# Long convolution, gate and MLP on one core: ssm_k transposed as words of two time steps, small tables first, another order in each group, one DMA per output tile

## The chip, the core and the metric

The kernel runs on one core of a Trainium2 chip. A core has a matrix engine (TensorE, "PE" in the profile, with its weight loads listed as "PEld"), a vector engine (VectorE, "DVE"), a scalar engine (ScalarE, "ACT") and a general engine (GpSimd, "POOL"), each with an instruction stream of its own, and queues from which data transfers (DMA) are issued ("SPq", "ACTq"). They run beside each other and wait for each other by semaphores. TensorE takes its operands from the on-chip memory SBUF and writes to PSUM[...]; DVE or ACT then bring a result from PSUM to SBUF, which is called an eviction here.

The metric is the time of one execution on the device in microseconds (us), the median of several runs: 208.96 us before the change. The profile is of one execution, and its span of 207.0 us is a little shorter than the time of a run.

## What is computed

With S = 2048 time steps, D = 512 channels and a hidden width of 1376, all tensors in bf16:

```python
def _A_ref(q, k, v, shift_k, ssm_k, ssm_D):        # q is layernorm(x)
    k_shift = sum over t of k_pad[:, t:t + S, :] * shift_k[:, ks - 1 - t]   # four taps
    kv = k_shift * v
    y = causal convolution of kv with ssm_k along the 2048 steps, by FFT of length 2 * S
    y = y + kv * ssm_D
    return q * y

x = A_q
h = x + _A_ref(_layernorm(x), A_k, A_v, A_shift_k, A_ssm_k, A_ssm_D)
h2 = h + relu(_layernorm(h) @ B_w1) @ B_w2
```

The kernel does the long convolution as a two-stage transform: 2048 steps are split into 32 rows of 64, a first stage transforms along one index, a second along the other. ssm_k and kv each go through both, are multiplied, and go back. Before a first stage, the data, which lie with channels on the partitions, are transposed so that time lies there.

## The kernel before

The kernel is written with a manual schedule: each engine runs its instructions in the order of the program text. These are the parts that matter for the change. The line numbers in the profile are those of the whole kernel.

The tables of the second stage (`cs`, `cc`; `cn` is the negative of `cs`) are sines, made by DVE (turns, in integers) and ACT (the sine). They come ahead of the small tables of the first stage (`f1f`):

```python
    for a, t in cs:                                   # two pieces, of 22 and 10 of the 32 indices
        ks = slice(a, a + t.shape[1])
        nc.vector.tensor_tensor(out=tsn[:, ks, :], ..., op=ALU.add)
        wrap(tsn[:, ks, :], 8192)                     # bitwise and, on DVE
        for dp in range(2):
            table((a, t), tsn, dp)                    # Sin, on ACT
    ...                                               # turns t1, t3; f1f and dsc by _sin on ACT
    cc_turns(0)                                       # two DVE instructions each
    cc_turns(16)
    ...
    for rg in range(DC):                              # on GpSimd: tap weights as diagonal matrices
        nc.gpsimd.tensor_tensor(out=wdiag[:, rg, :, :], ...)
        if rg == 1: ...                               # f1hi, f1lo from f1f, on GpSimd
    ...                                               # f2hi, f2lo, then cn = -cs in four pieces, on GpSimd
```

ssm_k (`sk`) is transposed as single 16-bit values, eight 128 x 128 transposes to a PSUM tile, and each tile is evicted by DVE ("D") or ACT ("A") in turn:

```python
    def to_rows(src, q, fl, eng):
        shape = [P, 8, P]
        pst = tap_bank(q % 5 - 3, shape, BF16, "pst") if q % 5 > 2 else place(shape, BF16, "pst")
        for i in range(8):
            nc.tensor.transpose(out=pst[:, i, :], in_=src[:, :, :, 8 * q + i], identity=ident[:])   # L268
        copy(eng, fl[:, :, :, 8 * q:8 * q + 8], pst[:].rearrange("p i (d g) -> p g d i", d=2))

    for q in range(8):
        to_rows(skv, q, kfl, "DADADADA"[q])
```

Then eight groups follow. In each, the four taps of a part of k are summed on TensorE into two PSUM banks of their own and multiplied by v on DVE (the product kv is written into the memory of `sk`), and one eighth of the first stage of ssm_k is computed and evicted into `a1k`:

```python
    def taps(c, h):
        ...                                           # 2 x 4 matmuls of 512 columns, L332; 2 products on DVE, L335

    for gb in range(8):
        taps(gb // 2, gb % 2)
        stage1(kfl, a1k, gb, ("AA", "AD")[gb % 2], pairs=(gb == 2))   # matmuls L289; two evictions
        if gb in (0, 1, 3, 5):
            cc_part()                                 # one sine of table cc, on ACT
    pl.pop("psT")                                     # the two tap banks become a fourth place
    places.append(pl.push("psX", space=PSUM))
    ring[:] = [1, 3, 2, 0]                            # order in which the places are used next
```

kv is then transposed as 32-bit words, each two time steps, so with half as many transposes. This is the form that the change takes for ssm_k too:

```python
    for q in range(8):
        pst = place([P, 4, P], F32, "pst2")
        for i in range(4):
            nc.tensor.transpose(out=pst[:, i, :], in_=kv32[:, 4 * q + i, :], identity=ident32[:])     # L369
        if "DADDADAD"[q] == "D":
            nc.vector.tensor_single_scalar(out=xfl32[:, :, :, ms], in_=pst[:].bitcast(I32)..., scalar=0,
                                           op=ALU.bitwise_or)                                         # L372
        else:
            for d in range(2):
                nc.scalar.copy(out=xfl[:, :, d, 8 * q:8 * q + 8]..., in_=src[:, d])                   # L378
```

The second stage of ssm_k (`ps2k`, L307 and L309) comes next, then the first stage of kv, the products, the way back, the gate and the MLP. At the end each output tile of 128 rows is stored by four DMAs of 32 rows; the last tile is computed and stored in two halves of 256 columns, whose DMAs alternate between two queues:

```python
                nc.vector.scalar_tensor_tensor(out=o[:, 0:w], in0=ps2[:, 0:w], ...)                   # L725
                for a, dst in enumerate(_tokens(out_d, t, 1)):
                    if parts > 1:
                        dst = bass.AP(tensor=dst.tensor, offset=dst.offset + w * h, ap=[[64 * D, 32], [1, w]])
                    eng = nc.scalar if parts > 1 and a % 2 else nc.sync
                    eng.dma_start(out=dst, in_=o[32 * a:32 * a + 32, 0:w])                            # L731
```

Of the kernel before, what the change touches and what calls it, by code (L numbers as in the profile page):

```python
# [9 lines left out]
ALU = mybir.AluOpType  # L10
BF16 = mybir.dt.bfloat16
# [45 lines left out]
def kernel(  # L57
# [122 lines left out]
    def wrap(t, M):  # L180
        nc.vector.tensor_single_scalar(out=t, in_=t, scalar=M - 1, op=ALU.bitwise_and)

    def table(piece, turns, dp):
        a, t = piece
        nc.scalar.activation(out=t[:, :, 64 * dp:64 * dp + 64], in_=turns[:, a:a + t.shape[1], :], func=ACT.Sin,
                             scale=hsc[:, dp:dp + 1], bias=hbi[:, dp:dp + 1])

    for a, t in cs:
        ks = slice(a, a + t.shape[1])
        nc.vector.tensor_tensor(out=tsn[:, ks, :], in0=ta[:, ks].unsqueeze(2).to_broadcast([P, t.shape[1], 64]),  # L190
                                in1=ta[:, 32:96].unsqueeze(1).to_broadcast([P, t.shape[1], 64]), op=ALU.add)
        wrap(tsn[:, ks, :], 8192)
        for dp in range(2):
            table((a, t), tsn, dp)
# [12 lines left out]
    cc_parts = [(p, dp) for p in cc for dp in range(2)]  # L207

    def cc_turns(a):
        part = tcs[:, a:a + 16, :]  # L210
        nc.vector.tensor_single_scalar(out=part, in_=tsn[:, a:a + 16, :], scalar=2048.0, op=ALU.add)
        wrap(part, 8192)

    def cc_part():
        p, dp = cc_parts.pop(0)
        table(p, tcs, dp)
# [8 lines left out]
    for f in (f2hi, f2lo):  # L225
        nc.gpsimd.memset(f[:], 0.0)

    for rg in range(DC):
        nc.gpsimd.tensor_tensor(out=wdiag[:, rg, :, :], in0=ident[:].unsqueeze(1).to_broadcast([P, KS, P]),
                                in1=wsh[:, rg, :].unsqueeze(2).to_broadcast([P, KS, P]), op=ALU.mult)  # L230
        if rg == 1:
            nc.gpsimd.tensor_copy(out=f1hi[:, 0:64], in_=f1f[:])
            nc.gpsimd.tensor_tensor(out=f1f[:], in0=f1f[:], in1=f1hi[:, 0:64], op=ALU.subtract)
            nc.gpsimd.tensor_copy(out=f1lo[:, 0:64], in_=f1f[:])
# [4 lines left out]
    for a, b in ((0, 8), (8, 16), (16, 22), (22, 32)):  # L239
        (ao, to), (ai, ti) = [[p for p in tab if p[0] <= a][-1] for tab in (cn, cs)]  # L240
        nc.gpsimd.tensor_single_scalar(out=to[:, a - ao:b - ao, :], in_=ti[:, a - ai:b - ai, :].bitcast(F32), scalar=-1.0,
                                       op=ALU.mult)

    def copy(eng, o, i):
        if eng == "A":
            nc.scalar.copy(out=o, in_=i)  # L246
        else:
            nc.vector.tensor_copy(out=o, in_=i)  # L248
# [12 lines left out]
    def tap_bank(i, shape, dtype, name):  # L261
        return psum_t.tile(shape, dtype, tag=f"pk{i}", name=name)

    def to_rows(src, q, fl, eng):
        shape = [P, 8, P]
        pst = tap_bank(q % 5 - 3, shape, BF16, "pst") if q % 5 > 2 else place(shape, BF16, "pst")
        for i in range(8):
            nc.tensor.transpose(out=pst[:, i, :], in_=src[:, :, :, 8 * q + i], identity=ident[:])  # L268
        copy(eng, fl[:, :, :, 8 * q:8 * q + 8], pst[:].rearrange("p i (d g) -> p g d i", d=2))

    def stage1(fl, a_out, gb, engs, pairs=False):

# [38 lines left out]


    kfl = early.tile([P, 64, 2, 64], BF16, name="kfl")
    skv = sk[:].rearrange("p c (a b) -> p c a b", b=64)
# [7 lines left out]


    kvp2 = sk[:].rearrange("p c t -> p (c t)").rearrange("p (m c a e) -> p m c a e", m=32, c=DC, e=2)
    ident32 = early.tile([P, P], F32, name="ident32")
    nc.gpsimd.tensor_copy(out=ident32[:], in_=ident[:])
# [34 lines left out]
    pl.pop("kvp")  # L361
    xfp = pl.push("xfp", side="right")
    xfl = xfp.tile([P, 64, 2, 64], BF16, name="xfl")
    kv32 = sk[:].rearrange("p c t -> p (c t)").bitcast(F32).rearrange("p (m x) -> p m x", m=32)
    xfl32 = xfl[:].rearrange("p g d n -> p (g d n)").bitcast(I32).rearrange("p (g d m) -> p g d m", g=64, d=2)
    for q in range(8):
        pst = place([P, 4, P], F32, "pst2")
        for i in range(4):
            nc.tensor.transpose(out=pst[:, i, :], in_=kv32[:, 4 * q + i, :], identity=ident32[:])  # L369
        ms = slice(4 * q, 4 * q + 4)  # L370
        if "DADDADAD"[q] == "D":
            nc.vector.tensor_single_scalar(out=xfl32[:, :, :, ms],  # L372
                                           in_=pst[:].bitcast(I32).rearrange("p m (d g) -> p g d m", d=2),
                                           scalar=0, op=ALU.bitwise_or)
        else:
            src = pst[:].rearrange("p m x -> p (m x)").bitcast(BF16).rearrange("p (m d g e) -> p d g m e", m=4, d=2, e=2)
            for d in range(2):
                nc.scalar.copy(out=xfl[:, :, d, 8 * q:8 * q + 8].rearrange("p g (m e) -> p g m e", e=2), in_=src[:, d])  # L378
    pl.pop("early")
    pl.pop("vp")  # L380
    slotB = pl.push("slotB")
# [440 lines left out]
```

## Time and profile before

| what | number |
|---|---|
| time, median of 3 runs (lowest to highest) | 208.96 us (208.96 to 210.03) |
| span of the profiled execution | 207.0 us |
| instructions in the profile | 4935 |
| transposes of ssm_k (L268) | 9.10 to 15.92 us |
| taps and first stage of ssm_k, eight groups | 15.75 to 36.1 us |
| transposes of kv (L369) | 36.28 to 40.17 us |
| second stage of ssm_k begins | 39.97 us |
| last product of the output (L725) | 202.58 to 203.06 us |
| DMAs of the output (L731) | 60 of 32 KB and 8 of 16 KB |

A line of the profile names the engine, the source line, the operation, the tile that is written and what it reads, then counts and times. "Idle" or "waited" is time in which an engine stood still, with the instruction or transfer that ended the wait. In a table of windows each row is a stretch of the span: its length, then the busy time and number of instructions of PE, PEld, DVE, ACT and POOL, then the granted clock of TensorE (1.00 is full), the busy share of the DMA engines and the GB/s.

### The profile page before, as it was taken

Reading aid. Unit: us, or ns where it says so; the run is one execution under the profiler, and the core shown is the slowest. Engines: PE = TensorE matmul, PEld = TensorE weight load, DVE = VectorE, ACT = ScalarE, POOL = GpSimd, SP = SyncE. Lnnn points to the kernel's source line nnn. Section 1 sums busy time; section 2 is a strip of 40 time slices with the busy share of each in tenths; the row PEclk is TensorE's granted clock in tenths of the full one; section 3 lists DMA queues with packets and bytes.
Section 4 is the critical chain, followed back from the end, with each engine's and each line's share of the span. In section 5 each row is a group of like instructions: output and inputs, shape, how many; then the busy total and the mean of one; then the engine's idle time right before and its main releaser. Section 6 shows DMA issues by size and latency. Waiting matters only on the chain.

```text
span 207.0 us, 4935 instructions
## 1 busy us (share of the span) xinstructions
PE 189.3 (91%) x1982; PEld 138.5 (67%) x1995; DVE 146.3 (71%) x236; ACT 130.2 (63%) x196; POOL 84.0 (41%) x121
## 2 busy tenths in 40 slices
PE   0299999999997999999999899999999999999991
PEld 0295554999876799987999787645565556544460
DVE  7996777867786998988995698978197317661131
ACT  2966988755696688886897975853680493026300
POOL 4199994000001999997759565120202001002000
PEclk9999999999999999999999999999999999999999
DMA  6999960000000005836892556772665412140022
GB/s 181 326 211 214 177 139 4 5 0 3 0 6 2 2 3 141 203 131 166 169 292 57 108 101 127 143 152 70 120 56 124 99 29 54 38 101 13 0 52 51
DMA packets 49510, 20.03 MB, mean 97 GB/s; under 512 B 44400, under 2 KB 47952, under 8 KB 49488
## 3 DMA queue, kind: packets, MB, share of 16 engines
q1 hardware_dynamic: 48768, 19.65, 44.6%
q8 instruction: 15, 0.25, 0.5%
q10 hardware_dynamic: 720, 0.07, 0.3%
q14 instruction: 7, 0.06, 0.1%
HBM read 7.08 MB, written 2.10 MB: 44 GB/s over the span
## 4 chain that ended last, share of the span: by engine, by line
PE 86%; DMA 4%; DVE 3%; ACT 3%; issue 1%; ACTq 0%
PE ps1m L691 19%; PE ps2m L721 18%; PE psy L439 7%; PE psi L586 7%; PE pkv L332 7%; PE ps L289 5%; DMA sk<-in_A_ssm_k_dram 4%; PE ps2k L307 4%; PE ps2k L309 4%; PE u L307 3%; PE pst L268 3%; PE u L309 3%; PE pz L664 3%; PE pst L369 2%; ACT a1x L246 1%; DVE a1x L248 1%
## 5 line engine op out<-in xcount | busy, mean ns | idle before, releaser
L706 ACT ACTIVATE h1T<-ps1m 128x512 bf16<-128x512 f32 (+1 forms) x44 | 25.7, 597 | 35.8 <-PE ps1m L691 35.7
L691 PE MATMUL ps1m<-xT,w 128*128 128x512 bf16 (+2 forms) x192 | 43.7, 365 | 0.4 <-DVE xT L637 0.4
L721 PE MATMUL ps2m<-w,h1T 128*128 128x512 bf16 (+3 forms) x181 | 40.2, 368 | 0.2
L664 PE MATMUL pz<-bd,ax 128*128 128x128 f32 x96 | 35.7, 410 | 0.0
L429 POOL TENSOR_TENSOR t<-usb,kf 128x320 fp32r<-128x320 f32 x32 | 28.2, 937 | 2.0 <-ACT usb L425 1.7
L429 DVE TENSOR_TENSOR t<-u,kf 128x704 fp32r<-128x704 f32 x32 | 26.7, 886 | 3.4 <-ACT usb L425 3.4
L725 DVE SCALAR_TENSOR_TENSOR o<-ps2m,rstd,xh 128x512 bf16<-128x512 f32 (+1 forms) x17 | 12.0, 717 | 21.9 <-PE ps2m L721 20.0
L721 PEld LDWEIGHTS <-h1T 128*128 128x128 bf16 (+1 forms) x187 | 16.2, 98 | 16.0
L530 POOL TENSOR_SCALAR rstd<-mv 128x4 f32<-128x4 f32 x8 | 2.5, 318 | 56.5 <-DVE mv L528 56.5
L691 PEld LDWEIGHTS <-w 128*128 128x128 bf16 (+1 forms) x192 | 15.9, 100 | 12.1 <-DVE xT L637 0.5
L664 PEld LDWEIGHTS pz<-bd,ax 128*128 128x128 f32 x96 | 18.6, 193 | 7.6
L635 DVE TENSOR_TENSOR qT<-pz,qT 128x1024 bf16<-128x1024 f32 x8 | 9.8, 1221 | 14.7 <-PE pz L664 7.3
L524 DVE BATCH_NORM_STATS2 st<-xh 128x6 f32<-128x512 bf16 x32 | 19.8, 678 | 0.0
L246 ACT CAST kf<-psy 128x512 fp32r<-128x512 f32 x30 | 17.5, 644 | 1.9 <-PE psy L439 0.2
L514 ACT ACTIVATE bd<-ecw,nbias 32x512 fp32r<-32x512 int32 x24 | 17.3, 719 | 0.6
L439 PE MATMUL psy<-t,ipos 128*128 128x512 f32 x48 | 16.0, 394 | 0.0
L332 PE MATMUL pkv<-kT,wdiag 128*128 128x512 bf16 x57 | 14.8, 381 | 0.4
L268 PE MATMUL pst<-ident,sk 128*128 128x128 bf16 x64 | 6.8, 303 | 9.1 <-DMA sk<-in_A_ssm_k_dram 9.1
L246 ACT CAST ax<-psi 128x1024 fp32r<-128x1024 f32 x13 | 12.6, 1014 | 3.5 <-PE psi L586 3.5
L586 PE MATMUL psi<-dre,kf 128*128 128x256 f32 x60 | 14.7, 287 | 0.0
L246 ACT CAST a1k<-ps 128x1024 fp32r<-128x1024 f32 x12 | 12.7, 1092 | 3.2 <-PE ps L289 3.2
L335 DVE TENSOR_TENSOR sk<-pkv,vT 128x512 bf16<-128x512 f32 x16 | 10.9, 690 | 5.3 <-PE pkv L332 5.3
(133 smaller groups left out, 417.3 us busy)
## 6 DMA issues: line engine op xcount, KB each, us to landing
sk<-in_A_ssm_k_dram SPq DMA_DIRECT2D x1, 2048.0 KB, 8.3
xh<-in_A_q_dram SPq DMA_DIRECT2D x16, 128.0 KB, 3.2
out_dram<-o SPq DMA_DIRECT2D x60, 32.0 KB, 1.6
w<-in_B_w_dram SPq DMA_DIRECT2D x1, 1376.0 KB, 6.6
w<-in_B_w_dram SPq DMA_DIRECT2D x1, 1280.0 KB, 7.8
xh<-xT SPq DMA_TRANSPOSE x8, 3.1
w<-in_B_w_dram SPq DMA_DIRECT2D x1, 96.0 KB, 6.6
kT<-in_A_k_dram SPq DMA_TRANSPOSE x4, 6.4
```

The costliest lines, as they stand in the source:

```text
L246: nc.scalar.copy(out=o, in_=i)
L307: nc.tensor.matmul(out=ps[:, kk, :], lhsT=at_k1(w_re, k1), rhs=a_in[:, k1, :], start=True, stop=False, skip_group_check=True)
L332: nc.tensor.matmul(out=pss[i][:], lhsT=wdiag[:, 2 * h + i, j, :], rhs=kT[c][:, 2 * h + i, 16 - j:CH + 16 - j], start=(j == 0), stop=(j == ...
L429: eng.tensor_tensor(out=t[:, :, j, :], in0=in0.unsqueeze(1).to_broadcast([P, 2, n, 2]), in1=kfr[:, :, j, ks], op=ALU.mult)
L439: nc.tensor.matmul(out=psy[:], lhsT=m_[:], rhs=t_.rearrange("p j k -> p (j k)"), start=first, stop=not first)
L514: nc.scalar.activation(out=bd[h][rows, :, :, rg, :], in_=ecw[q % 2][rows, :, 256 * h:256 * h + 256].rearrange("p b (j n) -> p b j n", n=32 ...
L524: nc.vector.bn_stats(out=st[:, i, :], in_=src[:, i, :])
L586: nc.tensor.matmul(out=banks[i // 2][:, i % 2, :], lhsT=kf[:, c, 4 * m:4 * m + 4, :].rearrange("p r k -> p (r k)"), rhs=d[:].rearrange("p ...
L664: nc.tensor.matmul(out=pz[:, il, :, a, :], lhsT=ax[:, 64 * rho + n2, :, :].rearrange("p d g -> p (d g)"), rhs=bd[h][:, rho, 4 * il + a, :, ...
L691: nc.tensor.matmul(out=ps1[fc][:fsz, 128 * ii.start:128 * ii.stop].rearrange("p (i t) -> p i t", t=P), lhsT=w1[:, c, fc * P:fc * P + fsz], ...
L706: nc.scalar.activation(out=h1T[:fsz, fc, :], in_=ps1[fc][:fsz, :], func=ACT.Relu)
L721: nc.tensor.matmul(out=ps2[:, 0:w], lhsT=h1T[:ksz, fc, i * P:(i + 1) * P], rhs=w2[:ksz, fc, ds], start=(fc == 0), stop=(fc == NFC - 1))
```

## The change

It has four parts.

1. ssm_k is transposed as words of two time steps, by the code that kv had; both now share `to_rows`. The identity in 32 bits is made earlier for it.
2. The small tables of the first stage are computed first, on DVE and ACT; GpSimd makes their split halves before the tap weights. Of the second stage's tables, only the larger piece of `cs` is finished ahead of the transposes. The sines of the smaller piece, the second `cc_turns` and one negation move behind the transposes and into the groups.
3. In each group the first stage comes ahead of the taps, and five of the eight groups split their two evictions between ACT and DVE (before, four). The sines are dealt out to six groups, and the ring of PSUM places behind the groups has another order.
4. Each output tile is stored by one DMA of all 128 rows on one queue; the two halves of the last tile likewise.

The purpose is less work in transposing and evicting ssm_k, an earlier start of the first stage, evictions of the last group that lie behind the taps, and fewer DMA issues. The core of the diff (the shared code of `to_rows` is cut, as it is what kv had):

```diff
-    for a, t in cs:
-        ...
+    def cs_turns(a, t):
+        ...                                          # the two DVE instructions of before
+    cs_turns(*cs[0])
+    for dp in range(2):
+        table(cs[0], tsn, dp)
+    cs_turns(*cs[1])
+    cc_parts = [(cs[1], tsn, dp) for dp in range(2)] + [(p, tcs, dp) for p in cc for dp in range(2)]
...
     cc_turns(0)
-    cc_turns(16)
...
+    ident32 = early.tile([P, P], F32, name="ident32")
+    nc.gpsimd.tensor_copy(out=ident32[:], in_=ident[:])
+    for rg in range(DC):
+        nc.gpsimd.tensor_tensor(out=wdiag[:, rg, :, :], ...)     # behind f1hi, f1lo, f2hi, f2lo
...
-    def to_rows(src, q, fl, eng):
-        shape = [P, 8, P]
-        ...
+    def to_rows(word, q, fl, eng):
+        shape = [P, 4, P]
+        ...
+        for i in range(4):
+            nc.tensor.transpose(out=pst[:, i, :], in_=word(4 * q + i), identity=ident32[:])
+        ...                                          # evictions as in the code for kv
...
     for q in range(8):
-        to_rows(skv, q, kfl, "DADADADA"[q])
+        to_rows(sk_word, q, kfl, "DADDADAD"[q])      # words 32 words apart: sk32[:, :, m]
+    cc_turns(16)
...
     for gb in range(8):
+        stage1(kfl, a1k, gb, ("AA", "AD")[gb in (1, 2, 4, 6, 7)], pairs=(gb == 2))
+        if gb in (0, 1, 2, 3, 4, 6):
+            cc_part()
+        if gb == 1:
+            negated(22, 32)
         taps(gb // 2, gb % 2)
-        stage1(kfl, a1k, gb, ("AA", "AD")[gb % 2], pairs=(gb == 2))
-        if gb in (0, 1, 3, 5):
-            cc_part()
...
-    ring[:] = [1, 3, 2, 0]
+    ring[:] = [1, 2, 0, 3]
...
-                for a, dst in enumerate(_tokens(out_d, t, 1)):
-                    if parts > 1:
-                        dst = bass.AP(tensor=dst.tensor, offset=dst.offset + w * h, ap=[[64 * D, 32], [1, w]])
-                    eng = nc.scalar if parts > 1 and a % 2 else nc.sync
-                    eng.dma_start(out=dst, in_=o[32 * a:32 * a + 32, 0:w])
+                dst = bass.AP(tensor=out_d.tensor, offset=out_d.offset + t * D + w * h, ap=[[16 * D, 4], [64 * D, 32], [1, w]])
+                nc.sync.dma_start(out=dst, in_=o[:, 0:w])
```

More of the change, by code (lines that the diff above doesn't have):

```diff
@@ L186, in table @@
                              scale=hsc[:, dp:dp + 1], bias=hbi[:, dp:dp + 1])
-    for a, t in cs:
[L189 to L194, printed above, removed]
     t1 = early.tile([P, 64], I32, name="f1_t")
@@ L206 @@
     _sin(dsc[:], t3[:], 64)
-    cc_parts = [(p, dp) for p in cc for dp in range(2)]
+    def cs_turns(a, t):
+        ks = slice(a, a + t.shape[1])
+        nc.vector.tensor_tensor(out=tsn[:, ks, :], in0=ta[:, ks].unsqueeze(2).to_broadcast([P, t.shape[1], 64]),
+                                in1=ta[:, 32:96].unsqueeze(1).to_broadcast([P, t.shape[1], 64]), op=ALU.add)
+        wrap(tsn[:, ks, :], 8192)
+    cs_turns(*cs[0])
[3 more added lines that the diff above has]
+    cc_parts = [(cs[1], tsn, dp) for dp in range(2)] + [(p, tcs, dp) for p in cc for dp in range(2)]
     def cc_turns(a):
@@ L214, in cc_part @@
     def cc_part():
-        p, dp = cc_parts.pop(0)
-        table(p, tcs, dp)
+        table(*cc_parts.pop(0))
     cc_turns(0)
-    cc_turns(16)
     f1hi = early.tile([P, 64], BF16, name="f1_hi")
@@ L226 @@
         nc.gpsimd.memset(f[:], 0.0)
[L228 to L234, printed above, removed]
+    nc.gpsimd.tensor_copy(out=f1hi[:, 0:64], in_=f1f[:])
+    nc.gpsimd.tensor_tensor(out=f1f[:], in0=f1f[:], in1=f1hi[:, 0:64], op=ALU.subtract)
+    nc.gpsimd.tensor_copy(out=f1lo[:, 0:64], in_=f1f[:])
     for f, g in ((f1hi, f2hi), (f1lo, f2lo)):
@@ L238, with negated @@
             nc.gpsimd.tensor_copy(out=g[rows, 64 * (rg % 2):64 * (rg % 2) + 64], in_=f[rows, :])
-    for a, b in ((0, 8), (8, 16), (16, 22), (22, 32)):
+    ident32 = early.tile([P, P], F32, name="ident32")
+    nc.gpsimd.tensor_copy(out=ident32[:], in_=ident[:])
+    for rg in range(DC):
+        nc.gpsimd.tensor_tensor(out=wdiag[:, rg, :, :], in0=ident[:].unsqueeze(1).to_broadcast([P, KS, P]),
+                                in1=wsh[:, rg, :].unsqueeze(2).to_broadcast([P, KS, P]), op=ALU.mult)
+    def negated(a, b):
         (ao, to), (ai, ti) = [[p for p in tab if p[0] <= a][-1] for tab in (cn, cs)]
@@ L242 @@
                                        op=ALU.mult)
+    negated(0, 8)
+    negated(8, 16)
+    negated(16, 22)
     def copy(eng, o, i):
@@ L262, in tap_bank @@
         return psum_t.tile(shape, dtype, tag=f"pk{i}", name=name)
-    def to_rows(src, q, fl, eng):
-        shape = [P, 8, P]
[L266 to L269, printed above, removed]
+    def to_rows(word, q, fl, eng):
+        shape = [P, 4, P]
+        pst = tap_bank(q % 5 - 3, shape, F32, "pst") if word is sk_word and q % 5 > 2 else place(shape, F32, "pst")
+        for i in range(4):
+            nc.tensor.transpose(out=pst[:, i, :], in_=word(4 * q + i), identity=ident32[:])
+        if eng == "D":
+            fl32 = fl[:].rearrange("p g d n -> p (g d n)").bitcast(I32).rearrange("p (g d m) -> p g d m", g=64, d=2)
+            nc.vector.tensor_single_scalar(out=fl32[:, :, :, 4 * q:4 * q + 4],
+                                           in_=pst[:].bitcast(I32).rearrange("p m (d g) -> p g d m", d=2),
+                                           scalar=0, op=ALU.bitwise_or)
+        else:
+            src = pst[:].rearrange("p m x -> p (m x)").bitcast(BF16).rearrange("p (m d g e) -> p d g m e", m=4, d=2, e=2)
+            for d in range(2):
+                nc.scalar.copy(out=fl[:, :, d, 8 * q:8 * q + 8].rearrange("p g (m e) -> p g m e", e=2), in_=src[:, d])
     def stage1(fl, a_out, gb, engs, pairs=False):
@@ L313, with sk_word @@
     kfl = early.tile([P, 64, 2, 64], BF16, name="kfl")
-    skv = sk[:].rearrange("p c (a b) -> p c a b", b=64)
+    sk32 = sk[:].rearrange("p c t -> p (c t)").bitcast(F32).rearrange("p (x m) -> p x m", m=32)
+    kv32 = sk[:].rearrange("p c t -> p (c t)").bitcast(F32).rearrange("p (m x) -> p m x", m=32)
+    def sk_word(m):
+        return sk32[:, :, m]
     for q in range(8):
-        to_rows(skv, q, kfl, "DADADADA"[q])
+        to_rows(sk_word, q, kfl, "DADDADAD"[q])
+    cc_turns(16)
     dre = consts.tile([P, 2, 2, 64], F32R, name="dre")
@@ L324 @@
     kvp2 = sk[:].rearrange("p c t -> p (c t)").rearrange("p (m c a e) -> p m c a e", m=32, c=DC, e=2)
-    ident32 = early.tile([P, P], F32, name="ident32")
-    nc.gpsimd.tensor_copy(out=ident32[:], in_=ident[:])
     def taps(c, h):
@@ L363 @@
     xfl = xfp.tile([P, 64, 2, 64], BF16, name="xfl")
-    kv32 = sk[:].rearrange("p c t -> p (c t)").bitcast(F32).rearrange("p (m x) -> p m x", m=32)
-    xfl32 = xfl[:].rearrange("p g d n -> p (g d n)").bitcast(I32).rearrange("p (g d m) -> p g d m", g=64, d=2)
     for q in range(8):
[L367 to L378, printed above, removed]
+        to_rows(lambda m: kv32[:, m, :], q, xfl, "DADDADAD"[q])
     pl.pop("early")
```

## The prediction

> **What bounds the kernel now.** I read the groups of instructions first, then the waits of TensorE, then the windows by stage, then single tiles and the tail of the timeline. The page's first part shows who is busy:
>
> ```profile
> PE 189.3 (91%) x1982; PEld 138.5 (67%) x1995; DVE 146.3 (71%) x236; ACT 130.2 (63%) x196; POOL 84.0 (41%) x121
> ```
>
> TensorE (PE) is busy 189.3 of 207.0 us, and its waits say where the other 18 us are. The columns are engine, what waited, for whom, total us, times, longest:
>
> ```profile
> PE pst L268 <- DMA sk<-in_A_ssm_k_dram: 9.1, 1, 9.1
> PE u L307 <- DVE a1x L248: 1.5, 1, 1.5
> PE ps1m L691 <- DVE xT L637: 0.4, 1, 0.4
> ```
>
> So the start is one wait for a load, and no wait after it is over 1.5 us. The windows by stage, with the busy time of each engine:
>
> ```profile
> 9.10:15.75 6.65, 6.65 (x64) 6.65 (x65) 6.26 (x7) 4.66 (x8) 6.04 (x10) 1.00 1.09 223
> 15.75:36.28 20.53, 19.90 (x540) 10.74 (x546) 15.13 (x21) 17.09 (x17) 17.41 (x29) 1.00 0.84 132
> 36.28:40.00 3.72, 3.71 (x33) 3.46 (x33) 3.57 (x5) 3.17 (x6) 0.00 (x0) 1.00 0.02 7
> ...
> 202.60:207.00 4.40, 0.00 (x0) 0.00 (x0) 0.46 (x1) 0.00 (x0) 0.00 (x0) 0.88 0.19 45
> ```
>
> The first three windows are all that the change touches ahead of 40 us, and PE is saturated in each: transposes of ssm_k (9.10 to 15.75), taps and first stage (to 36.28), transposes of kv (to 40.0). Everything from 40.0 to 202.6 is untouched and follows PE, so what the front gains or loses there should arrive at the end unchanged. The last window is 4.4 us with no PE work: the tail of the output.
>
> What paces the transposes matters most. The tile pst, both kinds (min/median/max ns), with the evictions:
>
> ```profile
> L268 PE MATMUL pst<-ident,sk x64: 230/314/351, 9.1 to 15.7; 128*128 128x128 bf16 x64
> ...
> L369 PE MATMUL pst<-ident,sk x32: 272/273/330, 36.3 to 39.9; 128*128 128x128 f32 x32
> L378 ACT COPY xfl<-pst x6: 586/591/616, 37.5 to 40.3; 128x512 bf16<-128x512 bf16 x6
> L372 DVE TENSOR_SCALAR xfl<-pst x5: 679/691/692, 37.3 to 40.2; 128x512 int32<-128x512 int32 x5
> L246 ACT COPY kfl<-pst x4: 1012/1017/1017, 11.1 to 16.0; 128x1024 bf16<-128x1024 bf16 x4
> L248 DVE COPY kfl<-pst x4: 1206/1217/1226, 11.4 to 15.2; 128x1024 bf16<-128x1024 bf16 x4
> ```
>
> The 16-bit transposes are not waiting for these evictions. Narrowed to 10 to 14.6 us, the timeline holds them as one run without a wait, and the starts of single ones in the trace are 106.7 ns apart from 9.24 until 14.68, then 67 to 102 ns apart. A 512-column matmul just after has its starts 216 ns apart, 54 ns per 128 columns. So the array ran at half speed for its first 5.6 us, whatever the page's granted clock (1.00) says.
>
> [...] our 32-bit transposes are 109 ns apart warm[...] cost goes by elements: 1024 halves take 1217 ns, 512 words 691 ns. [...] the 32 KB outputs land 1.6 us after issue (median).
>
> **The change part by part.**
> 1. Words of two time steps. Removed: 64 transposes of 16 bits, 4 DVE evictions of 1.22 us and 4 ACT ones of 1.02 us. Added: 32 transposes of 32 bits, 5 DVE evictions of 0.69 us and 6 ACT halves of 0.59 us, as kv has them already. Evictions fall from 8.9 us to 7.0 us, but they were not the pace. On PE, 32 at 109 ns are 3.5 us warm, and kv's whole phase took 3.7 us. But here the array is cold, and there are two cases.
>  - Case A: the 109 ns is two array passes per word (256 columns at the full rate; the duration of 273 ns is near the 276 ns of 256-column matmuls in the second stage). Then cold it is 213 ns: 26 transposes fit in the 5.58 us to 14.68, the other 6 take 0.65 us, and PE ends near 15.3 instead of 15.75. Last eviction: result at 15.5, 0.7 us on DVE, ACT alike: kfl complete at 16.25, stage 1 at 16.35.
>  - Case B: the 109 ns is the weight load, at a rate that the cold array does not change. Then 3.5 us end at 12.6, kfl is complete near 13.8, stage 1 begins near 13.9.
> 2. Tables first. The small tables of stage 1 leave DVE at about 4.2 us and ACT at 4.7. DVE is then through with the large tables at about 9.3 (before: 11.4, when its first eviction started), ACT at about 9.7 (before 10.7). It makes the evictions of part 1 prompt. The sine pieces of the smaller table (two of 0.87 us) go into the groups, where ACT had 17.1 of 20.5 us; with five of eight groups split between ACT and DVE, I sum 11.8 us copies plus 6.7 us sines for ACT, and 2.1 us per 2.45 us group for DVE. Tight, with perhaps 0.2 us of stall, but PE keeps the pace.
> 3. Stage 1 ahead of the taps. The order within a group costs PE nothing (2.45 us each, 2.9 once), but both ends change. At the start, the taps formerly filled the wait for the last evictions (they ran from 15.75, stage 1 at 17.57); now PE idles for it, about 0.9 us. At the end, kv's transposes wait for the last tap product. That chain is now: last tap matmul 0.38, product 0.69, start 0.15, against 0.22 for the next matmul had there been one: a gap of 1.0 us, where before stage 1 filled most of it (gap 0.43). In return kv's evictions no longer queue behind those of the last group (first one at 37.27, a us after its transposes): 32 x 0.109 = 3.5 against 3.68, which gives back 0.15 to 0.2.
>    Sum for the front, at the start of the second stage (39.97 before). Case A: PE's stream begins 0.6 later (16.35 against 15.75), the end gap adds 0.6, a possible stall 0.1, kv gives back 0.2: +1.1 us. Case B: stage 1 at 13.9 is 1.85 ahead of 15.75; the end gap and stall take 0.7, a still cold first group about 0.2, kv gives back 0.2: about -1.0 us.
> 4. One DMA per output tile. 64 KB or more in one issue instead of four (SP held 64 output issues of about 0.42 us each). In mid-kernel nothing waits for it. At the end it is on the path: the last product is done at 203.06, but SP is still issuing the half tile before it, then waits for a semaphore, and issues the last quarter at 204.38; it lands at 205.91 and the program ends 1.08 later. One issue at 203.1 with 128 rows of 512 bytes: taking 1.5 us as for the last quarter, plus 0.3 to 0.4 for the longer list of rows, it lands at about 205.0. Gain 0.9 us.
>
> **Sum.** A: 208.96 + 1.1 - 0.9 = 209.2. B: 208.96 - 1.0 - 0.9 = 207.1. I hold A for somewhat likelier, 6 to 4, as the duration of 273 ns is that of 256 columns: 0.6 x 209.2 + 0.4 x 207.1 = 208.3.
>
> **The rivals.** (i) Cost follows the evictions, and halving their elements shortens the phase to about the 3.7 us that kv's takes: front -2, in all about 206. The single starts speak against it: evenly spaced until 14.68, with no wait. (ii) The idle gap ahead of stage 1 falls into the warm-up and delays the full rate; each tap group run cold costs another 1.7 us: up to 210 or 211. For it: the gap lies just there. Against it:[...] in case A the array is warm by then. (iii) ACT or DVE becomes the bound in the groups with the sines and five split evictions: up to 0.5 us a group for some groups, 210. Their busy sums stay below PE's, so I give it little. (iv) The tail's single DMA is slower to land than I think: the gain shrinks to 0.3, so +0.6 on any case.
>
> **Range and chances.** The cases give 207.1 and 209.2, each with about 0.7 us of doubt from stalls, the moment of the warm-up and the tail; 206.6 to 210.0 holds them. Over 2% faster means below 204.8, more than even the first rival promises; over 2% slower means above 213.1, beyond the second and third together. So within 2% is nearly sure.
>
> **What would show it right or wrong.** Case A: word transposes 213 ns apart until about 14.7, then 109; stage 1 first at about 16.35; B: 109 throughout, stage 1 at 13.9. A gap of about 1.0 us before kv's first transpose, and no late first eviction of kv; second stage starting at 41.0 (A) or 39.0 (B). Groups still 2.45 us. At the end one SP issue right after the last product, and about 0.9 us less between the product and the end. I am wrong if PE's waits after 40 us change, if the groups stretch, or if the warm-up comes at another time.

## The result and the profile after

| what | before | after |
|---|---|---|
| time, median of 4 runs each (lowest to highest) | 208.96 us (208.20 to 210.03) | 211.97 us (211.37 to 212.19) |
| ratio after to before, with 95% interval | | 1.0136 [1.0086, 1.0185] |
| span of the profiled execution | 207.0 us | 209.7 us |
| first transpose of ssm_k | 9.10 us | 10.98 us |
| first group begins | 15.75 us (taps) | 18.32 us (stage 1) |
| second stage of ssm_k begins | 39.97 us | 42.74 us |
| last product of the output ends | 203.06 us | 206.14 us |
| from there to the end of the span | 3.92 us | 3.56 us |

The change made the kernel 3 us slower; 208.3 us, at most 210.0, was predicted. Here and below, medians are of all executions, and ratios leave out the few that took over 1.5% longer than the fastest of their kernel. The first part of the page after hardly differs from that of before:

```profile
span 209.7 us, 4806 instructions
...
PE 189.1 (90%) x1950; PEld 138.4 (66%) x1963; DVE 146.2 (70%) x238; ACT 128.3 (61%) x197; POOL 87.3 (42%) x121
```

TensorE has the same work (189.1 us) and DVE too; ACT has 1.9 us less. So the 2.7 us that the span has grown by are idle time of TensorE. Its waits in the first 45 us say where:

```profile
PE pst L273 <- POOL ident L236: 11.0, 1, 11.0
PE ps L302 <- DVE kfl L276: 0.9, 1, 0.9
PE pst L273 <- DVE sk L351: 0.8, 1, 0.8
```

The first line is the finding. Before, the one long wait was for the load of ssm_k and ended at 9.1 us. Now it ends at 11.0 us, and GpSimd ends it, with the identity matrix. The other two lines are the idle ends of the groups that part 3 of the prediction spoke of. The windows by stage, in the columns used above:

```profile
10.98:18.32 7.34, 6.46 (x33) 6.30 (x34) 3.62 (x6) 3.22 (x6) 7.26 (x6) 1.00 1.13 213
18.32:37.99 19.67, 19.29 (x537) 10.51 (x544) 17.00 (x22) 17.41 (x17) 13.02 (x21) 1.00 0.65 109
37.99:42.74 4.75, 3.96 (x34) 3.45 (x33) 3.68 (x6) 2.22 (x5) 0.00 (x0) 1.00 0.00 0
205.66:209.70 4.04, 0.00 (x0) 0.00 (x0) 0.48 (x1) 0.00 (x0) 0.00 (x0) 0.76 0.19 61
```

Between the first transpose and the first group there are 7.34 us (6.65 before), in the groups 19.67 us (before 20.08, both up to the start of the last matmul), from there to kv's first transpose 1.16 us (0.45 before) and kv's transposes with 3.59 us (3.69). Together: 1.88 later at the start, +0.69, -0.41, +0.71, -0.10, which is the +2.77 us of the second stage.

Why the identity is late is in the chain of work that ended last, here its beginning (start, duration, what):

```profile
3.28 0.57 ACT f_f L135 x2
3.91 0.25 POOL f_hi L228
4.23 1.74 POOL f_f L229
6.02 0.79 POOL f_lo L230
6.82 0.77 POOL f_hi L234
7.63 0.49 POOL f_hi L234
8.16 0.60 POOL f_hi L234
8.80 0.69 POOL f_hi L234
9.53 0.23 POOL f_lo L234
9.80 0.23 POOL f_lo L234
10.07 0.23 POOL f_lo L234
10.34 0.24 POOL f_lo L234
10.64 0.30 POOL ident L236
10.98 6.47 PE pst L273 x32
```

The 32-bit identity is the last of twelve GpSimd instructions, behind the split halves of the small table. Read the durations downwards: eight copies of one form (L234) take 0.49 to 0.77 us while they run before 9.5 us, and 0.23 to 0.24 us after it. The subtraction (L229) takes 1.74 us. In the kernel before it came later and took 0.31 us:

```profile
12.61 0.31 POOL L233 TENSOR_TENSOR f_f<-f_f,f_hi 128x64 f32<-128x64 f32 x1
```

What ran beside them on DVE in the kernel after, from the timeline (start, duration, instruction):

```profile
4.18 1.62 DVE L201 TENSOR_TENSOR w_ts<-w_ta 128x1408 int32<-128x1408 f32 x1
5.83 0.89 DVE L181 TENSOR_SCALAR w_ts<-w_ts 128x1408 int32<-128x1408 int32 x1
6.64 0.85 DVE L201 TENSOR_TENSOR w_ts<-w_ta 128x640 int32<-128x640 f32 x1
7.53 0.49 DVE L181 TENSOR_SCALAR w_ts<-w_ts 128x640 int32<-128x640 int32 x1
7.94 0.73 DVE L213 TENSOR_SCALAR w_tc<-w_ts 128x1024 int32<-128x1024 int32 x1
8.70 0.69 DVE L181 TENSOR_SCALAR w_tc<-w_tc 128x1024 int32<-128x1024 int32 x1
```

Add start and duration in both lists. DVE's instructions end at 5.80, 6.72, 7.49, 8.02, 8.67 and 9.39 us; GpSimd's long ones end at 5.97, 6.81, 7.59, 8.12, 8.76 and 9.49 us, each 0.09 to 0.17 us behind one of DVE's. After DVE's last one every copy has its short time again. It is not enough that DVE is busy: before, at 12.61 us, DVE was evicting from PSUM (11.36 to 14.88 us), and the subtraction was short (0.31 us). The author's reading of the two lists is that a slow instruction of GpSimd is held up until the DVE instruction beside it has ended; by what, the traces do not show. A run below tests whether DVE's table work is the cause, by taking it away.

At the other end, what the tail gained is small: 0.37 us. The last issue of SP starts at 206.17 us, right behind the last product, but the store lands 2.67 us later. Before, the last issue came 1.3 us after the product and its store landed after 1.50 us.

### The profile page after: what moved, and what is told of

Read it like the earlier page. It is cut to its first block, busy times and chain, and to the rows that moved or that the text cites. A ratio compares the mean times of both kernels' runs of the same rounds, so it can differ in the third digit from the quotient of the medians.

```text
span 209.7 us, 4806 instructions
## 1 busy us (share of the span) xinstructions
PE 189.1 (90%) x1950; PEld 138.4 (66%) x1963; DVE 146.2 (70%) x238; ACT 128.3 (61%) x197; POOL 87.3 (42%) x121
## 4 chain that ended last, share of the span: by engine, by line
PE 83%; DVE 6%; POOL 4%; ACT 3%; issue 2%; POOLq 0%; ACTq 0%
PE ps1m L696 19%; PE ps2m L726 18%; PE psy L444 7%; PE psi L591 7%; PE pkv L348 5%; PE pst L273 5%; PE ps L302 4%; PE ps2k L322 4%; PE ps2k L320 4%; PE u L320 3%; PE u L322 3%; PE pz L669 3%; DVE sk L351 2%; ACT a1x L251 1%; POOL f_hi L234 1%
## 5 line engine op out<-in xcount | busy, mean ns | idle before, releaser
L273 PE MATMUL pst<-ident,sk 128*128 128x128 f32 x64 | 10.3, 334 | 11.8 <-POOL ident L236 11.0
L273 PEld LDWEIGHTS pst<-ident,sk 128*128 128x128 f32 x64 | 9.7, 180 | 12.4 <-POOL ident L236 11.0
```

The costliest lines, as they stand in the source:

```text
L273: nc.tensor.transpose(out=pst[:, i, :], in_=word(4 * q + i), identity=ident32[:])
```

## The experiments

The theory for the start: the identity, held up on GpSimd by DVE's table work, costs most of the 3 us. Its rivals: the order in the groups (the idle gap, and through it a later full rate), or the words themselves. For the tail: the single store is slow as few DMA engines are busy with it (a share of 0.29 in the kernel after, as much as 4 to 5 of 16); its rival is that 128 rows in one store simply take that long. Ratios are to the kernel before, with the 95% interval. Last products and ends of spans are those of the profiled execution.

**The identity made early.** The kernel after, with one line moved up:

```diff
 # right behind the 16-bit identity
+    ident32 = early.tile([P, P], F32, name="ident32")
+    nc.gpsimd.tensor_copy(out=ident32[:], in_=ident[:])
 ...                                   # and no longer behind f2hi, f2lo
```

> The changed kernel, with one edit: the 32-bit identity is made right behind the 16-bit one, ahead of the tables' split halves in GpSimd's order. Theory 1 (the first transpose waited for that identity, and the half-speed time starts with the first transpose): first transpose near 9.1 us instead of 10.98, full speed near 14.8, first stage near 16.4 instead of 18.3, time 1.9 us below the changed kernel, so about 210.1. Theory 2 (the wait costs little, as the clock comes to full speed at a fixed moment): full speed still at 16.7, transposes end at 16.0, time about 1.2 to 1.4 below, 210.7. Theory 3 (the wait is off the path): time as the changed kernel, 212.0.

Measured: 209.04 us, ratio 1.0000 [0.9982, 1.0018]. The waits of TensorE:

```profile
PE pst L273 <- DMA sk<-in_A_ssm_k_dram: 8.9, 1, 8.9
PE ps L302 <- ACT kfl L282: 0.8, 1, 0.8
PE pst L273 <- DVE sk L351: 0.8, 1, 0.8
```

The first wait is again for the load, and the whole loss is gone: 1.36% of 209, 2.8 us by the ratios and 2.2 us by the two spans (1.9 was expected). GpSimd's split halves still take their slow times, but nothing waits for them. Only the place of one conversion of 0.3 us differs between the two kernels.

**DVE's table work taken away.** The kernel after, the identity at its late place; DVE fills the tables' angles with zeros instead of computing them, so the second stage's tables are not the right ones:

```diff
-        nc.vector.tensor_tensor(out=tsn[:, ks, :], in0=ta..., in1=ta..., op=ALU.add)
-        wrap(tsn[:, ks, :], 8192)
+        nc.vector.memset(tsn[:, ks, :], 0)
...
-        nc.vector.tensor_single_scalar(out=part, in_=tsn[:, a:a + 16, :], scalar=2048.0, op=ALU.add)
-        wrap(part, 8192)
+        nc.vector.memset(part, 0)
```

> The changed kernel without the turns of the second stage's tables: DVE fills them with zeros instead, which reads nothing from memory, so the tables and the output are not those of the reference. Theory (GpSimd's small instructions were held up by DVE's table instructions that run beside them, 1.73 us for one of 0.31): identity made near 7.4 us, first transpose when ssm_k lands, near 9.0. Rival (GpSimd's chain is simply that long): identity still near 10.6, first transpose at 11.

Measured: 209.08 us, ratio 0.9987 [0.9965, 1.001]. GpSimd's timeline, to be held against the chain of the kernel after:

```profile
3.91 0.24 POOL L225 CAST f_hi<-f_f 128x64 bf16<-128x64 f32 x1 [0.72 <-ACT f_f L135]
4.23 0.30 POOL L226 TENSOR_TENSOR f_f<-f_f,f_hi 128x64 f32<-128x64 f32 x1
4.60 0.24 POOL L227 CAST f_lo<-f_f 128x64 bf16<-128x64 f32 x1
4.77 1.04 POOL L231 COPY f_hi<-f_hi 32x64 bf16<-32x64 bf16 x4
5.86 1.04 POOL L231 COPY f_lo<-f_lo 32x64 bf16<-32x64 bf16 x4
6.96 0.29 POOL L233 CAST ident<-ident 128x128 f32<-128x128 bf16 x1
```

The same instructions in the same order start at the same 3.91 us, the subtraction takes 0.30 us instead of 1.73, and the identity is begun at 6.96 us instead of 10.64, 1.9 us ahead of the first transpose (8.84 us). DVE is not idle meanwhile: its zero fills run from 4.51 to 6.42 and from 6.58 to 7.49 us, and they do not slow GpSimd. So the twelve instructions alone would have been harmless. The late place and DVE's computing of the tables beside it were both needed for the loss.

**Single parts added to the kernel before.** Part 3 alone (stage 1 ahead of the taps, with the ring that goes with it):

```diff
-        taps(gb // 2, gb % 2)
         stage1(kfl, a1k, gb, ...)
         ...
+        taps(gb // 2, gb % 2)
-    ring[:] = [1, 3, 2, 0]
+    ring[:] = [1, 2, 0, 3]
```

> The kernel before with the order of part 3 alone (first stage ahead of the taps in each group, and the ring order that goes with it; evictions and sines dealt out as before). Theory: the wait for the last eviction of ssm_k is laid open (+1.3 us: first stage at about 17.1 where the taps ran at 15.75), the gap ahead of kv's transposes grows by 0.6 to 0.7, kv gives back 0.15: together +1.8, about 210.8. Rival: the evictions of the last group, now behind the taps, pay for it: 0 to +0.5.

Measured: 210.59 us, ratio 1.0088 [1.0064, 1.0113]. TensorE now waits 1.1 us for the last eviction ahead of stage 1 and 0.9 us for the last product ahead of kv's transposes. The order costs 1.8 us by itself (by the ratio; 1.4 us by the medians), about what was expected. So the rival has a share in the truth: the order is a loss, only not the one that the change shows, since with the identity early the other parts make up for it.

Part 1 alone (`to_rows` with words and the eviction of the diff, identity early):

> The kernel before with part 1 alone: ssm_k transposed as words, the 32-bit identity made early so that nothing waits for it; tables, order and output as before. Theory (two array passes per word, half speed for the first 5.6 us or so): 213 ns each at first, the transposes end about 0.45 us earlier than before, 208.5. Rival (fewer eviction elements shorten the phase): 206.5 or less. Second rival (DVE is busy with tables until 11.4, so the first evictions of smaller tiles block): 209 or more.

Measured: 208.79 us, ratio 0.9993 [0.9974, 1.0011]. The transposes end at 15.26 us, where the 16-bit ones end at 15.92; the gain that this should give is not to be told from zero. In this profile TensorE stood still once for 1.4 us in stage 1, with no wait that the profile names.

Part 4 alone (one DMA per output tile):

> The kernel before with part 4 alone: one DMA per output tile. By the two profiles, last product to end is 3.92 us before and 3.53 after: if that is the whole effect, -0.4 us, 208.6. By the prediction's estimate of the landing, -0.9, 208.1. If fewer issues also help in the middle, more than 1 us. If the longer landing eats the gain, 0.

Measured: 208.82 us, ratio 0.9988 [0.9968, 1.0008]; 3.56 us from the last product to the end, 0.36 us less than before, as in the change itself. In the time this is not to be told from zero.

**The other order, on the mended change.** The identity early, and the taps ahead of stage 1 again, with the ring of before:

> The changed kernel with the identity made first and with the taps ahead of the first stage again; no dummy matmuls. Theory (the order of part 3 costs 1.0 to 1.4 us, as from the third run against the kernel before and from the two kernels with dummies): about 1.1 us below the run with the identity first, 207.9. Rival (in the slow-clock case the order costs nothing, as the groups wait elsewhere, for instance for DVE's late table): 208.8 to 209.1.

Measured: 208.31 us, ratio 0.9967 [0.995, 0.9984]; against the same kernel with stage 1 first (209.04) it is 0.7 us faster, where 1.1 was expected. With this order the taps fill the wait for the last evictions at the start of the groups: TensorE's waits of 0.8 us there and of 0.8 us ahead of kv's transposes become one of 0.4 us for DVE in the groups and one of 0.2.

**The array at full speed.** How much of the first phase is the half speed of TensorE? 22 dummy matmuls of 512 columns, ahead of the transposes, while the load is under way. In each of the six profiles with them, their starts go from 427 to 216 ns apart before the first transpose.

```diff
+    warm = kfl[:].rearrange("p g d n -> p (g d n)")[:, 0:512]
+    nc.vector.memset(warm, 0.5)
+    wps = psum_t.tile([P, 512], F32, tag="pk0", name="wps")
+    for _ in range(22):
+        nc.tensor.matmul(out=wps[:], lhsT=warm[:, 0:P], rhs=warm, start=True, stop=True)
```

In the kernel before:

> The kernel before, with 22 dummy matmuls of 512 columns ahead of the first transpose (on a constant tile, into the first tap bank, read by nobody), so that TensorE is at full speed when ssm_k lands. Theory (the 16-bit transposes at full speed[...] about 0.09 us each, as in the late part of the profiles): transposes end near 15.0 instead of 15.8, time -0.7, 208.4. Rival (half speed was their pace[...]): they end near 14, time -1.8, 207.3. Second rival: no change, as something else is the bound.

Measured: 210.85 us, ratio 1.0116 [1.006, 1.0173]: a miss. The 16-bit transposes were then about 90 ns apart, only a little closer than at half speed (107 ns), and had to wait 0.8 us for DVE's first eviction; the phase ended at 15.85 us, no earlier than before. And in the profiled execution, the longest of the four, this happened (wait of TensorE, then two windows with the granted clock third from the end):

```profile
PE ps L295 <- issue: 2.5, 1, 2.5
```

```profile
20.38:22.76 2.38, 0.20 (x24) 0.09 (x12) 0.38 (x1) 1.04 (x1) 2.38 (x1) 1.00 1.10 115
22.76:26.17 3.41, 3.10 (x15) 1.15 (x15) 1.92 (x2) 2.26 (x2) 3.41 (x3) 0.50 1.79 237
```

TensorE stood still for 2.5 us in the middle of stage 1 with nothing in the profile to wait for ("issue"), and from 22.76 us on the clock was 0.50 for 3.41 us. Such standstills, 0.2 to 2.5 us, are in seven of these profiles at different places. A transfer of instructions (16 KB) covers the first 1.1 us of this one, but in the other six the last such transfer had ended 0.1 to 1.2 us before. Why they come is open, and so is why the other three executions, of which there is no profile, were 1.5 to 2 us slower than the kernel before.

In the kernel before with part 1 (words, identity early):

> Words alone (part 1, identity made early, tables and order as before) with the same 22 dummy matmuls. Theory (words at full speed take 0.109 us; the tables, still first on DVE until 11.4 us, hold up the first eviction): transposes end near 13.5 to 14.5, time -1.3 to -2 against the words alone, 207.0. Rival (the evictions are not in the way): they end at 12.7, time -3, 206. Second rival (the array's speed does not matter for words): no change, 208.8.

Measured: 207.70 us, ratio 0.9942 [0.9923, 0.9961]. Between this run and the last, only the words differ and the time falls by 3.2 us, of which that standstill may be a part. The words came 113 ns apart, but waited 1.7 us for DVE, busy with the large tables (they come first here).

In the change with the identity early, where the large tables come later:

> The changed kernel with the identity made first, and the 22 dummy matmuls. Theory (half speed is what makes the words slow, two passes each; the tables are out of the way): transposes 109 ns apart from the start, end near 12.7, first stage near 13.7 instead of 15.9, time -2.2 against the run without dummies, 206.8. Rival (dummies only move work, or half speed comes back in the gap ahead of the first stage): less than 0.7 us.

Measured: 207.47 us, ratio 0.9918 [0.9894, 0.9942]; transposes 8.95 to 12.78 us, without that wait. Against the same kernel without dummies (8.91 to 15.06 us) the half speed of the first phase cost 2.3 us in the transposes, and 1.7 us in the time by the ratios, where 2.2 was expected.

The same with the taps ahead of stage 1:

> As the previous kernel, but with the taps ahead of the first stage in each group again (evictions and sines dealt out as in the change). Theory (the order of part 3 lays open two waits): taps from about 13.0, gap ahead of kv's transposes 0.4 instead of 1.2, time another 1.0 to 1.4 below, about 205.6. Rival (the tap weights or loads of k and v are not there so early, and the groups wait): as the previous kernel, or slower.

Measured: 206.48 us, ratio 0.9900 [0.9866, 0.9935]. Waits of TensorE in the first 45 us:

```profile
PE wps L111 <- DVE kfl L108: 1.4, 1, 1.4
PE pkv L353 <- DVE sk L356: 1.2, 1, 1.2
PE pst L279 <- DVE sk L356: 0.3, 1, 0.3
```

The first line is the dummies' own start. The wait ahead of kv's transposes is down to 0.3 us, and the one ahead of stage 1 is gone. But the second group of taps now waits 1.2 us for a product on DVE, which first has the two instructions of `cc_turns(16)` to do (13.55 to 15.78 us). Against the version with stage 1 first the gain is 1.0 us by the medians and 0.2% by the ratios, whose intervals overlap, so the expected 1.0 to 1.4 us are not shown. This version is faster than both kernels, by 2.5 us (2.1 by the ratio) and by 5.5 us.

**The tail.** The kernel before, with the DMAs of the last two tiles on two queues in turn (before, only the last one):

```diff
-                    eng = nc.scalar if parts > 1 and a % 2 else nc.sync
+                    eng = nc.scalar if t >= NT - 2 and a % 2 else nc.sync
```

> The kernel before, where the four DMAs of each of the last two output tiles alternate between the two queues (before, only those of the last tile's halves did). Theory (before, the end waits for SyncE's issues, each transfer being quick): the last product's DMAs are issued at once, last landing about 0.8 us earlier, 208.3. Rival (the landing is a fixed cost after the last product): no change, 209.1.

Measured: 208.25 us, ratio 0.9973 [0.9952, 0.9994]; 3.20 us from the last product to the end.

Why is the single DMA slow to land? Part 4 alone, but with the rows of a tile going to 128 consecutive rows of the output (the output's rows are permuted, so it is not the reference's). The outermost dimension of the list is then 128 instead of 4:

```diff
-                dst = bass.AP(..., offset=out_d.offset + t * D + w * h, ap=[[16 * D, 4], [64 * D, 32], [1, w]])
+                dst = bass.AP(..., offset=out_d.offset + t * P * D + w * h, ap=[[D, P], [1, w]])
```

> The kernel before with part 4 alone, as in the run of one DMA per tile, but the rows of a tile go to 128 consecutive rows of the output (so the rows of the output are permuted): the outermost dimension of the transfer is 128 instead of 4. Theory (the transfer was slow to land[...]): DMA share in the tail rises above 0.25, the landing comes 1.5 to 1.7 us after the issue instead of 2.7, from the last product to the end 2.5 instead of 3.55 us, time near 207.8. Rival (128 rows on 128 partitions, or the issue itself, cost the time, however they are spread): 3.5 us from product to end, time 208.8 as with part 4 alone.

Measured: 207.60 us, ratio 0.9898 [0.9854, 0.9943]; 2.42 us from the last product to the end, where part 4 alone had 3.56. Short windows while the last store moves, in the kernel after and then here (last columns: granted clock, DMA share, GB/s):

```profile
207.80:208.20 0.40, 0.00 (x0) 0.00 (x0) 0.00 (x0) 0.00 (x0) 0.00 (x0) 0.50 0.29 87
```

```profile
203.80:204.00 0.20, 0.00 (x0) 0.00 (x0) 0.00 (x0) 0.00 (x0) 0.00 (x0) 1.00 0.56 166
204.00:204.20 0.20, 0.00 (x0) 0.00 (x0) 0.00 (x0) 0.00 (x0) 0.00 (x0) 1.00 0.58 162
```

With the outermost dimension of 4 the DMA engines stand at a mean share of 0.29, as much as 4 to 5 of 16, at 87 GB/s, and the store's packets take 0.77 us (207.69 to 208.46); with 128 they reach 0.56 to 0.58 and 166 GB/s and are through in 0.36 us. A packet of 512 bytes takes about 27 ns in both, so it is the number under way at a time that differs. The rest of the late landing has two more parts. In the kernel after, the store of the tile before (packets from 205.20 to 206.95 us), that of the first half (to 207.69) and the last one stand in a row, so the last one's packets, which start 1.17 us after the issue where nothing is ahead, start 1.52 us after it. Here they start 0.83 us after it. The answer for the output tensor gives the landing:

```profile
L728 SPq DMA_DIRECT2D out_dram<-o x17: 330/333/571, 137.9 to 203.0; - x17
...
DMA to landing us min/median/max: 1.5/1.7/2.0
```

The issue is shorter too (333 ns against 537). The rival falls: 128 rows as such are not slow. That the share follows the outermost dimension is the author's reading of these two kernels: the rows of a tile also lie side by side in memory in this run; the equal packet times speak against that as the cause, but no run separates the two. Of the 2.0 us gained on the kernel before, 1.50 are the tail's in the two profiles (3.92 to 2.42), 1.14 of them against part 4 alone; the rest lies ahead of the last product and is not explained by this edit.

**All of it together.** First with `cc_turns(16)` moved into the third group, four DMAs per tile, and the last two tiles on two queues:

> The kernel with taps first and dummy matmuls, with two more edits: the second turns of table cc on DVE move from ahead of the groups into the third group, and the output goes by four DMAs a tile as before, the last two tiles' on two queues. Theory: the wait of 1.2 us of the second tap group for DVE goes, and about 0.8 us of the tail: 206.5 - 1.0 - 0.7 = 204.8. Rival (the groups then wait for the loads of v, or stand still for instructions): 206.

Measured: 207.84 us, ratio 0.9941 [0.9916, 0.9966]: a miss, by 3 us. The longest wait of TensorE in the front:

```profile
PE pkv L352 <- DVE sk L355: 2.2, 1, 2.2
```

The taps wait for DVE, which in the middle of the groups has these two large instructions to do ahead of its product. Then with `cc_turns(16)` left where the change has it, the rest unaltered:

> The version of taps first with the array warmed (206.48), with the tail of four DMAs per tile of which those of the last two tiles alternate between two queues, and cc_turns(16) left where the change put it. Theory (the late cc_turns alone spoiled the combined version): no wait of the taps for DVE over 1.5 us in the groups, last product near 204.6 or wherever the clock puts it, 3.2 us from product to end, time near 206.2. Rival (four DMA issues per tile or the two queues cost time in mid-kernel that the one-DMA form saved): 206.5 to 207.8.

Measured: 206.52 us, ratio 0.9849 [0.9791, 0.9907]; the wait of the taps is 1.2 us again, and 3.11 us go from the last product to the end. So the late `cc_turns` had spoiled the combined version. By its time (206.22 without one execution of 210.79) it is level with the version that has one DMA per tile (206.48), and by its ratio it may be half a per cent better; the intervals overlap, so which tail is better for it stays open.

## Why the prediction was wrong

The step that failed is the start of the words, in parts 1 and 2. Part 1 let them start when the load lands: "26 transposes fit in the 5.58 us to 14.68". Part 2 counted when the tables leave DVE and ACT, and left GpSimd out, though the diff puts the identity, which every word transpose needs, at the end of GpSimd's list there. What the runs showed in its place is a wait for that identity. Missing was a term of +1.88 us in the profile (10.98 against 9.10); by the ratios, moving the identity is worth 2.8 us. In the profiles of the change and of the kernel with the identity early, the second stage begins 2.42 us apart: 2.08 are the start of the words (10.98 and 8.91), and 0.35 their phase (7.33 and 6.99 us), as half speed lasted 5.6 us in one and 5.0 in the other. What remains up to 2.8 us is not settled; from profile to profile half speed lasts 2.7 to 5.7 us.

A sum of GpSimd's durations from the profile of before would not have been enough, as it gives an identity at about 7 us, which is what the run without DVE's computing shows. One had to see that those instructions now run beside DVE's tables and not after them.

Point by point for the rest:

- Part 1, case A (213 ns): right. The starts of the words are 213 ns apart from 11.26 us until 16.59 and then, after one of 130 ns, 109 to 111 ns. Case B, an assumption of the author's, held at 4 in 10, is refuted: at half speed the words are 213 ns apart, not 109. That a word is two passes was the author's reading of two durations (273 and 276 ns); no run shows it. Rival (i) did not happen: at half speed no word waits for an eviction. Case A's stage 1 was to begin 7.25 us after the first transpose; 7.34 us were measured.
- Full rate: 5.6 us after the first transpose (5.7 before). It came 1.8 us later only as the transposes did, so rival (ii), the gap that delays it, did not happen.
- Part 2, prompt evictions: DVE was through with its tables at 9.39 us (9.3 predicted), and in the kernel with the identity early the first eviction waits for transposes. The stall of 0.1 us in the groups did not come; the groups became 0.41 us shorter together (2.45 us each and one of 2.83, where before there were one of 2.91, one of 2.56 and one of 2.50). Rival (iii) did not happen either.
- Part 3, both ends: an idle wait of 0.9 us at the start, as predicted, and at the end 1.16 us from the start of the last tap matmul to kv's first transpose, where the chain of the prediction (0.38, 0.69 and 0.15) gives 1.22; its "1.0" is this less the 0.22 of a next matmul. The last lines ahead of kv's transposes in the timeline:

```profile
36.46 1.90 PE L348 MATMUL pkv<-kT,wdiag 128*128 128x512 bf16 x7
36.59 1.12 ACT L251 CAST a1k<-ps 128x1024 fp32r<-128x1024 f32 x1 [0.22 <-PE ps L302]
36.64 1.23 DVE L253 CAST a1k<-ps 128x1024 fp32r<-128x1024 f32 x1
37.78 1.32 DVE L351 TENSOR_TENSOR sk<-pkv,vT 128x512 bf16<-128x512 f32 x2
39.15 1.40 PEld L273 LDWEIGHTS pst<-ident,sk 128*128 128x128 f32 x13 [1.28 <-DVE sk L351]
```

  In the last group, DVE takes a share of the eviction (1.23 us) first, so the products start at 37.78 us. But the second one, which kv's transposes wait for, starts at 38.41 us, right behind the last tap matmul (which ends at 38.37 us), so the eviction did not lengthen the gap. kv gave back 0.10 us (0.15 to 0.2 predicted).
- The sum for the front was +1.1 us for case A. Without the missing term the profile has +0.69 - 0.41 + 0.71 - 0.10 = +0.89 us. The times of case A hold for the words. The kernel with the identity early is the one that was predicted, and it took 209.04 us against the 209.2 of case A, but that is partly luck: in its profile the second stage begins only 0.36 us later than before (40.32 against 39.97), not 1.1, and the tail gained 0.37 us, not 0.9. The two misses cancel.
- Part 4, the tail: "plus 0.3 to 0.4 for the longer list of rows, it lands at about 205.0" was an estimate with no run behind it, and mis-sized. The issue came as predicted, right behind the product. The landing took 2.67 us, not 1.8 to 1.9. 0.37 us was gained, not 0.9: rival (iv), as the run with 128 as the outermost dimension shows. The longer list was not the cost (there, too, it has 128 rows); the transfer at a DMA share of 0.29 was, and with it the stores ahead, behind which the last one's packets started 1.52 us after the issue instead of 1.17.
- "Everything from 40.0 to 202.6 is untouched": nearly. The +2.77 us of the second stage became +3.08 at the last product, a drift of 0.3 us that no run here explains.

## What to carry to other kernels

When a change gives an instruction a new operand, follow the engine that makes that operand, and ask what runs beside it: here a subtraction of 128x64 on GpSimd took 1.73 us beside DVE's computing of the tables and 0.30 us without it. A lone conversion that a main phase depends on belongs at the head of its engine's list: here its place was worth 2.8 us by the ratios. Of a store in one DMA, ask how many DMA engines are busy with it: here the share was 0.29 with an outermost dimension of 4 and 0.56 to 0.58 with 128, and from the last product to the end it took 3.56 and 2.42 us. Four small stores on two queues took 3.20 us.

## What the hardware showed

- GpSimd beside DVE's table work: 0.30 us became 1.73 us for a 128x64 subtraction, and 0.23 us up to 0.77 us for a 32x64 copy, the long ones each ending 0.09 to 0.17 us after a DVE instruction did. Beside DVE's evictions from PSUM the subtraction took 0.31 us, and beside its zero fills a copy at most 0.24.
- A 32-bit 128x128 transpose takes 213 ns from start to start at half speed and 109 ns at full speed, a 16-bit one with its values 128 bytes apart 107 ns and about 90 ns. So here full speed halved the words' time and took a sixth off the 16-bit form.
- TensorE, with nothing but transposes to do, came to full speed after 2.7 to 5.7 us.
- The last store, 64 KB in 128 rows: its packets took 0.77 us with an outermost dimension of 4 and 0.36 us with 128; from issue to landing it took 2.67 us, queued behind two others, and 1.5 us.
- Standstills of TensorE of 0.2 to 2.5 us that no wait explains, once with 3.41 us at half clock from near its end.
